# Two heads in one kernel (a Fourier mixing layer and a state-space convolution): seeds of two chunks of tables made together, inputs of the odd outputs made one group sooner

## The chip, the cores and the metric

The kernel runs on one core of one Trainium2 chip. The metric is the device time of one execution, in microseconds (us). A core has five engines that each take their instructions in a fixed order: PE (TensorE, matrix products), DVE (VectorE), ACT (ScalarE), POOL (GpSimd) and SP (SyncE, which here only issues transfers). They wait for each other through semaphores, and 16 DMA engines move data between DRAM (HBM) and the core's memory.

## The reference

Two independent heads are computed and laid side by side. Head A is the real part of a two-dimensional Fourier transform, by matrices; head B is a causal convolution along the sequence, by Fourier transforms of twice the length.

```python
# A: x is 1 x 2048 x 512
a = einsum("bsd,ed->bse", x, dft_hid_re);  b = einsum("bsd,ed->bse", x, dft_hid_im)
yA = einsum("ts,bse->bte", dft_seq_re, a) - einsum("ts,bse->bte", dft_seq_im, b)
# B: u is 1 x 2048 x 512; A, C are 512 channels x 128 modes, dt has 512 channels
P = exp((A * dt[:, None])[:, :, None] * arange(2048))         # 512 x 128 x 2048
K = 2 * einsum("dn,dnl->dl", C, P).real                       # a filter of 2048 taps per channel
yB = irfft(rfft(u, 4096) * rfft(K, 4096))[:2048] + u * D_skip
out = concatenate([yA, yB], axis=-1)                          # 1 x 2048 x 1024
```

## The kernel before, in words

**One program, planned ahead.** Two classes, `Fnet` (head A) and `Ssm` (head B), hold tasks written as generators. Each step of a task names an engine, a cost in us and perhaps an urgency; `Plan` runs the tasks against these costs while the program is built and so fixes the order of instructions on each engine. On the chip nothing is reordered: an instruction whose input is late holds up all that stand behind it on its engine. The constants at the file's end (`GROUP_US`, `AHEAD_US`, `SEEDS`, `ARGS` and others) and the costs in the steps therefore change the order, though they compute nothing.

**Head A.** The rows of x are folded by symmetry, so that 2048 output rows come in four quarters t = 0..3 (t = 2 and 3 hold the odd rows) with a sine part (c = 1) and a cosine part (c = 0). For each (t, c), called a group, `matmuls` and `sums` (L519 to L523) multiply the folded x by four "quads" of the sequence matrix S. A quad (`load_quad`) is 1 MB: a `base` of 256 KB and three `slots` tiles of 256 KB, which DVE turns into a bf16 `rest` (L414, L419). The loading of quads is paced by `loads`: quad n is held until `GROUP_US*(n//4) + QUAD_US*(n%4) - AHEAD_US`. After both parts of a quarter, `outputs` (L619, L620) applies the hidden matrix, 16 pairs of matmuls per quarter, and `evacuate` copies to `y` and stores `out_ya`. For t = 2 and 3 other foldings of x are needed: `load_odd(k)`, k = 0..3, loads x again into a `slots` tile, subtracts twice (L307), and `folded` makes the sine input "os" and the cosine input "oc" (L321 or L323, then L328). They overwrite the tiles of "es" and "ec" of quarter 1, so all four calls are made in `finish` of group (1, 0), after both parts of quarter 1 are through.

**Head B, tables.** The powers P are never formed in full. For 16 chunks of 32 channels, DVE makes two tables by repeated doubling: `tables1` (low powers times C, tiles t1) and `tables2` (powers of 32, tiles t2, with squares from ACT). All start from "seeds" `cs`, the powers 1, 2, 4, ... of one step, made per chunk: `load_par` fetches the chunk's parameters, `seed_args` computes arguments (five ACT copies L993 and L995, two DVE instructions L997 and L999), then ACT takes an exponential (L1003) and three sines (L1005, L1007, L1009), with a table load of ACT ahead of the exponential and ahead of the first sine; `seeds` multiplies them on DVE (L1018). The tile "seed" has one buffer, `cs` two.

**Head B, from tables to output.** `taps` (L1158) contracts t1 with t2 on PE to 2048 taps for each channel of a chunk; two chunks go through a first Fourier stage (`stage1_k`, L1234) to a spectrum `xk` in DRAM. The spectrum `xu` of u is made early. Channels are then taken in five units of 128, 128, 128, 64 and 64 (units 0 to 4), in quarters: 4, 4, 4, 2 and 2 of them. A quarter loads pieces of `xu` and `xk`, goes through PE (L1399), ACT (L1424), DVE (the complex product, two of L1429 and two of L1431) and PE again (L1445), and is stored to `zs`; `inverse` loads `zs`, runs L1516 and stores `out_yb`. Unit 4, the last 64 channels, needs the last two chunks: its spectrum does not go through DRAM, but stays in the tables' memory (`last_stage1_k`, L1206 and a DVE transpose L1212, then the DVE product L1417 and a transpose L1496). Unit 3 is marked late: DVE takes its products after the last table.

**The names used below.** "The end of tables" is the end of the last DVE instruction of L953, the last half of t1 of chunk 15. Behind it only head B's last units remain.

Of the kernel before, what the change touches and what calls it, by code (L numbers as in the profile page):

```python
# [57 lines left out]
ARGS = 0.3  # L58
# [138 lines left out]
class Fnet:  # L197
# [11 lines left out]
    def __init__(self, tc, ctx, plan, x, wT, sT, out):  # L209
# [5 lines left out]
        self.slots = Ring(self.slots_all[:, n] for n in range(SLOTS))  # L215
        self.ys = Sem(STAGED)
# [11 lines left out]
        self.checked, self.checks, self.odd_ev = Event(), 36, Event()  # L228
# [66 lines left out]
    def load_odd(self, k):  # L295
        nc = self.nc
        yield self.bases
# [12 lines left out]
        yield from self.folded("oc", k, raw[:, 0], raw[:, 1], OP.subtract, None if k else 1)  # L310
        self.ssm.give_tile(self.slots, raw)

    def folded(self, name, k, left, right, op, sign=None):

        nc, v, minus = self.nc, self.nc.vector, name[1] == "s"
# [4 lines left out]
        if sign is None:  # L320
            v.tensor_tensor(y, left, right, op=op)  # L321
        else:
            v.scalar_tensor_tensor(y, right, self.sign[:, sign:sign + 1], left, op0=OP.mult, op1=OP.add)  # L323
        n = 1 if minus else 2
# [45 lines left out]
    def loads(self, b):  # L370
# [3 lines left out]
        for n, i in enumerate(self.quads):  # L374
# [77 lines left out]
    def spare(self):  # L452
# [4 lines left out]
        self.ssm.give_tile(self.ssm.big, flat[:, :2048])  # L457
        self.ssm.give_tile(self.ssm.mid, flat[:, 2048:])
# [69 lines left out]
    def finish(self, t, c, bank, both):  # L528
# [186 lines left out]
class Ssm:  # L715


    def __init__(self, tc, ctx, plan, nd, ldt, dsk, uG, f1u, f1k, w2, ia, ib, ibl, out):
# [18 lines left out]
        self.t1_half, self.half_taps, self.last_xt, self.last_k, self.last_ib = (Event() for _ in range(5))  # L737
# [96 lines left out]
    def load_tables(self):  # L834
# [11 lines left out]
        first = self.tab.tile([128, 4, CHUNK], F32, name="par", bufs=2)  # L846
        yield self.pars
        self.rest, self.par = rest, {0: first}
# [56 lines left out]
    def setup_rest(self):  # L905
# [8 lines left out]
        self.par[1] = self.tab.tile([128, 4, CHUNK], F32, name="par", bufs=2)  # L914
        yield "act", act(4 * CHUNK)
        self.nc.scalar.activation(self.par[1], par[:, :, :CHUNK], AF.Copy)
# [9 lines left out]
    def load_par(self, ck):  # L926
        if ck == 1:
            yield self.par1_ev
            return
        yield self.par_ev  # L930
        yield self.pars
        self.par[ck] = self.tab.tile([128, 4, CHUNK], F32, name="par", bufs=2)
        o = CHUNK * ck - FIRST
        yield "dma", load(2 * CHUNK)
        self.nc.sync.dma_start(self.par[ck], self.par_dram[:, :, o:o + CHUNK])
# [45 lines left out]
    def seed_args(self, ck, box, ev):  # L981

        a, v = self.nc.scalar, self.nc.vector
        if ck:
# [640 lines left out]
```

## Time and profile before

| what | value |
|---|---|
| median of 3 runs (lowest, highest) | 488.81 us (486.59, 490.38) |
| time of the profiled execution | 487.21 us |
| span of the profiled execution, first to last instruction | 485.1 us |
| granted PE clock, mean | 0.961 |
| busy: PE, DVE, ACT | 397.4, 428.5, 347.4 us |
| DMA | 110.49 MB, mean 228 GB/s |

The span is what the trace shows; the time has 2.1 us more around it. Busy is time in which an engine worked; the rest of the span it waited. "A <- B" names what an engine waited for. In a timeline a row is a stretch of equal instructions: start in us from the span's start, length in us, engine, line, operation, output tile <- input tiles, shapes, count, and in brackets the idle time ahead of it with what ended it. A float32 matmul of the program stands as two in the trace.

### The profile page before, as it was taken

How to read it: one execution, taken by the hardware profiler on the slowest of the kernel's cores; microseconds unless marked ns; L12 is line 12 of the kernel's file. 1: busy time of each engine (PE TensorE's matmuls, PEld its weight loads, DVE VectorE, ACT ScalarE, POOL GpSimd, SP SyncE). 2: the span in 40 equal slices, each digit the busy share in tenths (PEclk: the TensorE clock that was granted, in tenths of full speed). 3: DMA queues.
4: the chain of work that ended last, by engine and by line, in shares of the span. 5: the costliest groups of instructions: out<-in, count | busy, mean ns of one | idle time of the engine just before them, and what ended most of it. 6: DMA issues, size and time to landing. Idle time of an engine off the chain costs nothing. (4 is left out here: it accounts for less than half of the span.)

```text
span 485.1 us, 13793 instructions
## 1 busy us (share of the span) xinstructions
PE 397.4 (82%) x5744; PEld 213.3 (44%) x5778; DVE 428.5 (88%) x732; ACT 347.4 (72%) x687; POOL 1.3 (0%) x15
## 2 busy tenths in 40 slices
PE   4548958999998695798897799998976989886593
PEld 3113214354534352453445254644343556665383
DVE  3999997989999999989999999999999999982433
ACT  1529899899998884669858988887897754633331
POOL 1000000000000000000000000000000000000000
PEclk9988987999999998999999999999999999997888
DMA  8998894895976379994986279449301995998674
GB/s 308 340 295 297 291 330 139 295 329 189 278 281 214 139 204 322 336 286 154 284 258 235 61 232 309 141 119 329 87 3 49 251 296 165 288 253 195 220 198 112
DMA packets 130546, 110.49 MB, mean 228 GB/s; under 512 B 57136, under 2 KB 101552, under 8 KB 129968
## 3 DMA queue, kind: packets, MB, share of 16 engines
q1 hardware_dynamic: 122512, 106.55, 70.1%
q10 hardware_dynamic: 7968, 3.02, 2.4%
q8 instruction: 47, 0.77, 0.7%
q14 instruction: 19, 0.16, 0.1%
HBM read 77.11 MB, written 32.44 MB: 226 GB/s over the span
## 5 line engine op out<-in xcount | busy, mean ns | idle before, releaser
L944 DVE TENSOR_TENSOR prod<-tables,cs 128x1024 f32<-128x1024 f32 (+4 forms) x160 | 124.6, 798 | 3.7 <-ACT tables L1087 2.3
L619 PE MATMUL f<-p,w 128*128 128x512 f32 x128 | 67.7, 610 | 8.9 <-ACT y L645 5.8
L953 DVE TENSOR_TENSOR tables<-prod 128x512 f32<-128x512 f32 (+4 forms) x160 | 74.0, 477 | 0.8
L443 ACT ACTIVATE slots<-rest 128x1536 f32<-128x1536 bf16 x32 | 47.4, 1480 | 16.3 <-DVE rest L414 13.8
L414 DVE TENSOR_TENSOR rest<-slots,base 128x512 bf16<-128x512 f32 (+2 forms) x52 | 53.8, 1034 | 1.9 <-DMA slots<-in_sT 1.8
L1158 PE MATMUL f<-tables 128*32 128x96 f32 x2048 | 47.0, 247 | 9.2 <-ACT big L808 2.8
L1158 PEld LDWEIGHTS f<-tables 128*32 128x32 f32 x2048 | 42.6, 110 | 18.6 <-issue 6.0
L520 PE MATMUL f<-base,es 128*128 128x512 f32 x64 | 36.9, 660 | 15.5 <-ACT es L331 7.2
L1110 DVE TENSOR_TENSOR tables<-tables,cs 128x1024 f32<-128x1024 f32 x32 | 38.0, 1220 | 0.0
L619 PEld LDWEIGHTS f<-p,w 128*128 128x128 f32 x128 | 22.5, 189 | 32.0 <-issue 16.0
L520 PE MATMUL f<-base,ec 128*128 128x512 f32 x64 | 34.3, 618 | 1.2 <-ACT big L1424 0.8
L523 PE MATMUL f<-rest,xi 128*128 128x512 bf16 x87 | 26.2, 397 | 5.7 <-ACT xi L273 2.5
L1399 PE MATMUL f<-big,w 64*32 64x256 f32 (+1 forms) x768 | 23.7, 380 | 6.1 <-DMA big<-xk 5.1
L1424 ACT ACTIVATE big<-f 128x1024 f32<-128x1024 f32 x22 | 21.9, 1020 | 7.8 <-PE f L1399 3.9
L808 ACT ACTIVATE big<-f 128x512 f32<-128x512 f32 x39 | 21.0, 588 | 7.2 <-PE f L1516 7.2
L523 PE MATMUL f<-rest,xr 128*128 128x512 bf16 x92 | 25.2, 379 | 0.6 <-DVE rest L414 0.4
L967 ACT ACTIVATE tables<-tables 128x1024 f32<-128x1024 f32 x16 | 16.8, 1050 | 10.5 <-PE f L1158 8.4
L1234 PE MATMUL f<-ks,f1k 32*128 32x512 f32 (+1 forms) x224 | 22.4, 499 | 2.3 <-ACT ks L1182 1.5
L523 PEld LDWEIGHTS <-xi 128*128 128x128 bf16 x96 | 9.5, 101 | 30.1 <-issue 21.8
L520 PEld LDWEIGHTS f<-base,es 128*128 128x128 f32 x64 | 11.8, 203 | 24.6 <-ACT es L331 10.5
L1023 ACT ACTIVATE cs<-cs 128x352 f32<-128x352 f32 x32 | 15.8, 530 | 9.0 <-DVE cs L1018 8.9
L1399 PEld LDWEIGHTS f<-big,w 64*32 64x32 f32 x768 | 14.0, 111 | 15.9 <-issue 10.6
(187 smaller groups left out, 732.7 us busy)
## 6 DMA issues: line engine op xcount, KB each, us to landing
slots<-in_sT SPq DMA_DIRECT2D x31, 768.0 KB, 6.0
xu<-big SPq DMA_DIRECT2D x16, 512.0 KB, 4.1
base<-in_sT SPq DMA_DIRECT2D x31, 256.0 KB, 6.2
xk<-big SPq DMA_DIRECT2D x7, 1024.0 KB, 6.8
big<-xu SPq DMA_DIRECT2D x11, 512.0 KB, 7.7
big<-xk SPq DMA_DIRECT2D x11, 512.0 KB, 7.3
zs<-mid SPq DMA_DIRECT2D x10, 512.0 KB, 6.2
big<-zs SPq DMA_DIRECT2D x10, 512.0 KB, 7.0
```

What stands on the lines that cost most here:

```text
L414: return v.tensor_tensor(rest[:, lo:hi:step], raw[:, lo:hi:step], base[:, None, :].to_broadcast([128, n, DM]), op=op)
L443: nc.scalar.activation(raw, rest, AF.Square, accum_out=self.stat[:, n:n + 1])
L520: nc.tensor.matmul(out, x[:, cols], base, start=k == 0, stop=False)
L523: nc.tensor.matmul(out, still[:, cols], rest[:, h], start=False, stop=k == 3 and h == 2)
L619: nc.tensor.matmul(ps, self.w[k][:, cols], self.p[t, c][:, d], start=k == 0, stop=False)
L944: self.nc.vector.tensor_tensor(p.rearrange("p k d c m -> p k (d c) m"), src.rearrange("p d c l -> p (d c) l")[:, None, :, rows].to_broadca ...
L953: self.nc.vector.tensor_tensor(dst[:, :, :, rows], p[:, 0], p[:, 1, :, ::-1], op=OP.add)
L1110: self.nc.vector.tensor_tensor(self.top[:, :, k, ::1 - 2 * k, 16:32], t[:, :, :, 1:32:2], cs[:, k, 5, :, :, None].to_broadcast([128, CHUNK ...
L1158: nc.tensor.matmul(ps[32 * j:32 * j + 32, i], t1[:, d, c], t2[:, :, d, c], start=c == 0, stop=c == 1, tile_position=(0, 32 * j))
L1234: nc.tensor.matmul(to, self.f1k[r, STEPS[a]], taps, start=a == 0, stop=a == 4, tile_position=(32 * j, 0))
L1399: nc.tensor.matmul(both[:, :, c], self.w2[rows, R * q + r, xx, 32 * c:32 * c + 32], xs[rows, r, xx], start=True, stop=True, tile_position= ...
L1424: a.activation(flat[:, 1024 * m:1024 * m + 1024], p.rearrange("p b d -> p (b d)"), AF.Copy)
```

## The change

- **Seeds of two chunks together.** A table `PAIRS` groups the 16 chunks as 0; 1 and 2; 3 and 4; ...; 13 and 14; 15. `load_par` and `seed_args` run once for a pair, on tiles of double width; `seeds` still runs once per chunk, on half of the pair's tile. The tiles "par" and "seed" are twice as large. `f1k_last` has no buffer of its own any more; it takes the buffer "square" after that one's last use.
- **x for odd t a group sooner.** `load_odd` is now spawned in `finish` of group (1, 1), when only "es" is free. It makes "os" as before. "oc" has no free tile yet: its first DVE step works in place in the `slots` tile, the result is stored to DRAM (`oc`, 256 KB for each k), and a new task `load_oc`, spawned in `finish` of group (1, 0), loads it into a `y` tile and makes the rest.
- **Pace of S and urgencies.** `GROUP_US` 42 to 43, `AHEAD_US` 25 to 35; `ARGS` 0.3 to 1; `SEEDS` 0.5 to 1.5; planned cost of `taps` 2.45 to 2.8 (last chunk 1.25 to 1.42 a half).

```diff
-ARGS = 0.3
+ARGS = 1
     def load_odd(self, k):
         nc = self.nc
+        yield self.even_ev
         yield self.bases
...
         yield from self.folded("os", k, raw[:, 1], raw[:, 0], OP.add, None if k else 0)
-        yield from self.folded("oc", k, raw[:, 0], raw[:, 1], OP.subtract, None if k else 1)
+        yield "dve", dve(512)
+        if k:
+            nc.vector.tensor_tensor(raw[:, 0], raw[:, 0], raw[:, 1], op=OP.subtract)
+        else:
+            nc.vector.scalar_tensor_tensor(raw[:, 0], raw[:, 1], self.sign[:, 1:2], raw[:, 0], op0=OP.mult, op1=OP.add)
+        yield "dma", load(256)
+        nc.sync.dma_start(self.oc[k], raw[:, 0])
         self.ssm.give_tile(self.slots, raw)
+        self.plan.set(self.oc_ev[k])
+
+    def load_oc(self, k):
+        yield self.oc_ev[k]
+        yield self.ys
+        y = self.pool.tile([128, DM], F32, name="y", bufs=STAGED)
+        yield "dma", load(256)
+        self.nc.sync.dma_start(y, self.oc[k])
+        yield from self.fold("oc", k, y)
...
             elif n == 16:
+                self.plan.set(self.even_ev)
                 yield self.odd_ev
...
-            if (t, c) == (1, 0):
-                self.plan.spawn(self.load_odd(k), 0)
+            if t == 1:
+                self.plan.spawn(self.load_odd(k) if c else self.load_oc(k), 0)
...
+    def take_pair(self, g):
+        first, m = PAIRS[g]
+        self.pair[g] = self.tab.tile([128, 4, 2 * CHUNK], F32, name="par", bufs=2)[:, :, :m * CHUNK]
+        for j in range(m):
+            self.par[first + j] = self.pair[g][:, :, CHUNK * j:CHUNK * j + CHUNK]
...
-    def seed_args(self, ck, box, ev):
+    def seed_args(self, g, box, ev):
...
-        s = self.tab.tile([128, 3, 11, CHUNK], F32, name="seed")
+        s = self.tab.tile([128, 3, 11, 2 * CHUNK], F32, name="seed")[:, :, :, :w]
...
-    def seeds(self, ck, s):
+    def seeds(self, g, j, s):
         yield self.css
+        s = s[:, :, :, CHUNK * j:CHUNK * j + CHUNK]
...
-        self.plan.put(self.res)
+        if j == PAIRS[g][1] - 1:
+            self.plan.put(self.res)
...
-            yield "pe", 2.45, None, 257
+            yield "pe", 2.8, None, 257
...
-        self.f1k_last = self.tab.tile([128, 3, 128], F32, name="f1k_last")
+        yield self.squared
+        self.f1k_last = self.tab.tile([128, 512], F32, name="square")[:, :384].rearrange("p (e s) -> p e s", e=3)
...
+PAIRS = ((0, 1), *((n, 2) for n in range(1, 15, 2)), (15, 1))
-FIRST_TABLE, T1, SEEDS = 0.01, 0.005, 0.5
+FIRST_TABLE, T1, SEEDS = 0.01, 0.005, 1.5
-GROUP_US, QUAD_US, AHEAD_US = 42, 11, 25
+GROUP_US, QUAD_US, AHEAD_US = 43, 11, 35
```

The planner's new order moves much more than the diff says. Three places follow. The changed file is longer, so its lines have other numbers there: L944, L953, L1158, L1206, L1212, L1399, L1429, L1431 of before are L980, L989, L1200, L1248, L1254, L1442, L1472, L1474.

The first place is DVE at the end of tables. Before, from the last table (the second row here) on:

```order
L944 TENSOR_TENSOR prod<-tables,cs 128x1024
L953 TENSOR_TENSOR tables<-prod 128x32x16
L1429 TENSOR_TENSOR mid_106<-slots 128x512
L1212 STREAM_TRANSPOSE tables<-f_4486 128x2x8x32
L1431 TENSOR_TENSOR slots<-slots 128x2x256
L1212 STREAM_TRANSPOSE tables<-f_4487 128x2x8x32
L1429 TENSOR_TENSOR mid_106<-slots 128x512
L1431 TENSOR_TENSOR slots<-slots 128x2x256
L1212 STREAM_TRANSPOSE tables<-f_4553 128x2x8x32
L1212 STREAM_TRANSPOSE tables<-f_4588 128x2x8x32
L1429 TENSOR_TENSOR slots<-big_103 128x512
L1431 TENSOR_TENSOR big_103<-big_103 128x2x256
```

With the change, at the same place (the last table is the sixth row):

```order
L1254 STREAM_TRANSPOSE tables<-f_4482 128x2x8x32
L980 TENSOR_TENSOR prod<-tables,cs 128x1024
L1254 STREAM_TRANSPOSE tables<-f_4529 128x2x8x32
L989 TENSOR_TENSOR tables<-prod 128x32x16
L980 TENSOR_TENSOR prod<-tables,cs 128x1024
L989 TENSOR_TENSOR tables<-prod 128x32x16
L1472 TENSOR_TENSOR slots<-slots 128x512
L666 COPY y<-f_4266 128x256
L1474 TENSOR_TENSOR slots<-slots 128x4x128
L1472 TENSOR_TENSOR slots<-slots 128x512
L1474 TENSOR_TENSOR slots<-slots 128x4x128
```

A shape ending in 2x256 is a quarter of unit 2, one in 4x128 a quarter of unit 3: before, the last two quarters of unit 2 stand behind the end of tables; now they stand ahead of it, and two of unit 4's transposes too, while the copy of head A's last output (L666, before at L639) has gone behind it.

The second place is PE ahead of the last chunk's taps (the row with L1158 or L1200). Before, head A had ended earlier:

```order
L1158 MATMUL f_4369<-tables 32x96 x64
L1399 MATMUL f_4375<-slots,w_95 32x2x128 x16
L1399 MATMUL f_4411<-slots,w_95 32x2x128 x16
L1206 MATMUL f_4486<-ks,f1k_last 128x256 x2
L1206 MATMUL f_4487<-ks,f1k_last 128x256 x2
```

With the change, directly ahead of the last chunk's taps:

```order
L646 MATMUL f_4266<-p_3685,w_438 128x512
L647 LDWEIGHTS v_481
L647 MATMUL f_4266<-low_3706,v_481 128x512
L646 MATMUL f_4266<-p_3141,w_507 128x512
L647 LDWEIGHTS v_555
L647 MATMUL f_4266<-low_3239,v_555 128x512
L1442 MATMUL f_4534<-slots,w_98 32x2x64 x32
L1442 MATMUL f_4563<-slots,w_98 32x2x64 x32
L646 MATMUL f_4266<-p_3141,w_585 128x512
L647 LDWEIGHTS v_610
L647 MATMUL f_4266<-low_3239,v_610 128x512
L1200 MATMUL f_4573<-tables 32x96 x64
```

The matmuls of head A's last output tile (L646, L647, before at L619, L620) now stand between the taps of chunks 14 and 15, and the first quarter of unit 3 (shape 32x2x64) has come ahead of the last taps.

The third place is SP where x for odd t is loaded. Before:

```order
L935 DMA par<-par_dram 128x4x32
L764 DMA ib<-in_ib 128x2048
L304 DMA slots<-in_x 128x512 x3
L304 DMA base<-in_x 128x512
L304 DMA slots<-in_x 128x512 x3
L304 DMA base<-in_x 128x512
L935 DMA par<-par_dram 128x4x32
L648 DMA out_ya<-y 128x512
L796 DMA xk_83<-big_102 4096x1x64
L304 DMA slots<-in_x 128x512 x3
L304 DMA base<-in_x 128x512
```

With the change, at the last two of the four x (their loads are above these rows; L319 stores oc, L329 loads it again, L423 and L425 load the first quads of S for odd t):

```order
L319 DMA oc<-slots 128x512
L675 DMA out_ya<-y 128x512
L1410 DMA big_106<-xu 128x8x128
L319 DMA oc<-slots 128x512
L1410 DMA big_106<-xk_86 128x8x128
L675 DMA out_ya<-y 128x512
L329 DMA y<-oc 128x512
L423 DMA base<-in_sT 128x512
L425 DMA slots<-in_sT 128x3x512
L329 DMA y<-oc 128x512
L423 DMA base<-in_sT 128x512
L425 DMA slots<-in_sT 128x3x512
```

Four stores and four loads of 256 KB have come into the SP queue, two of the loads behind a gather of `xk` (512 KB) and ahead of the quads that the odd groups wait for.

More of the change, by code (lines that the diff above doesn't have):

```diff
@@ L456, in spare @@
         flat = self.slots_all.rearrange("p n h t -> p (n h t)")
[L457 to L458 removed]
+        n = 3 * DM * SLOTS // 2048
+        for m in range(n):
+            self.ssm.give_tile(self.ssm.big, flat[:, 2048 * m:2048 * m + 2048])
+        for m in range(2 * n, 3 * DM * SLOTS // 1024):
+            self.ssm.give_tile(self.ssm.mid, flat[:, 1024 * m:1024 * m + 1024])
     def first(self):
@@ L931, in load_par @@
         yield self.pars
[L932 to L935, printed above, removed]
+        self.take_pair(g)
+        first, m = PAIRS[g]
+        o = CHUNK * first - FIRST
+        yield "dma", load(2 * m * CHUNK)
+        self.nc.sync.dma_start(self.pair[g], self.par_dram[:, :, o:o + m * CHUNK])
     def mul(self, name, src, rows, seed):
@@ L1065, in tables1 @@
             self.nc.scalar.activation(t[:, :, :, 0].rearrange("p d c -> p c d"), self.par[n][:, 2:4], AF.Copy)
-            self.plan.put(self.pars)
+            if any(n == first + m - 1 for first, m in PAIRS):
+                self.plan.put(self.pars)
             for j in range(4):
```

59 lines of the change are left out of this document (34 added, 25 removed).

## The prediction

> **What bounds the kernel now.** First the busy time by engine on the page, then the same by stage. In the stage rows the columns are PE, PEld, DVE, ACT and POOL busy (with instruction counts), granted PE clock, DMA share and GB/s.
>
> ```profile
> PE 397.4 (82%) x5744; PEld 213.3 (44%) x5778; DVE 428.5 (88%) x732; ACT 347.4 (72%) x687; POOL 1.3 (0%) x15
> 40.00:400.00 360.00, 314.25 (x3857) 154.88 (x3888) 346.00 (x591) 299.44 (x593) 0.00 (x0) 0.98 0.71 223
> 388.10:423.90 35.80, 32.08 (x736) 21.86 (x737) 35.11 (x66) 20.81 (x36) 0.00 (x0) 1.00 0.81 249
> 425.80:485.10 59.30, 40.56 (x1256) 32.20 (x1256) 25.77 (x35) 18.76 (x31) 0.00 (x0) 0.86 0.74 195
> ```
>
> From 40 to 400 us DVE works 346.00 of 360 us. PE and ACT have 46 and 61 us to spare. So up to the end of tables the kernel is DVE's queue, and any work or wait put into that queue is paid in full. From 425.8 us on DVE works 25.77 of 59.30 us: that is another regime, which I call the tail. Next the DVE timeline, for where the regimes meet and for the prices of what the order moves across that point:
>
> ```profile
> 403.28 0.42 DVE L639 COPY y<-f 128x256 f32<-128x256 f32 x1
> 407.10 0.67 DVE L1429 TENSOR_TENSOR mid<-big 128x512 f32<-128x512 f32 x1
> ...
> 409.75 0.15 DVE L481 TENSOR_SCALAR small<-small 1x2 f32<-1x2 f32 x1
> 425.09 0.69 DVE L953 TENSOR_TENSOR tables<-prod 128x512 f32<-128x512 f32 x1
> 430.10 2.07 DVE L1212 STREAM_TRANSPOSE tables<-f 128x512 f32<-128x512 f32 x2
> 450.26 0.69 DVE L1429 TENSOR_TENSOR prod<-tables 128x512 f32<-128x512 f32 x1 [10.12 <-ACT tables L1424]
> ```
>
> The tables end at 425.09 + 0.69 = 425.78 us; the tail is 485.10 - 425.78 = 59.3 us. The row at 450.26 shows DVE idle for 10.12 us: in the tail the products go round PE, ACT, DVE and PE. PE's timeline says what that takes.
>
> ```profile
> 423.95 1.53 PE L1158 MATMUL f<-tables 128*32 128x96 f32 x64 [0.86 <-DVE tables L953]
> 430.00 1.96 PE L1399 MATMUL f<-big,w 64*32 64x256 f32 x64
> 442.11 1.56 PE L1445 MATMUL f<-slots,ia 32*64 32x256 f32 x21 [3.69 <-issue]
> 447.44 2.59 PE L1399 MATMUL f<-tables,w 64*32 64x128 f32 x165
> 457.72 2.00 PE L1445 MATMUL f<-prod,ia 32*64 32x256 f32 x28 [2.92 <-issue]
> 460.45 1.98 PE L1516 MATMUL f<-big,ib 128*64 128x128 f32 x16 [0.73 <-ACT prod L808]
> 465.37 1.09 PE L1516 MATMUL f<-big,ib 128*64 128x128 f32 x16
> 466.39 1.21 PE L1445 MATMUL f<-tables,ia 32*64 32x256 f32 x32
> 467.31 1.16 PE L1445 MATMUL f<-prod,ia 32*64 32x256 f32 x32
> 468.39 1.09 PE L1516 MATMUL f<-slots,ib 128*64 128x128 f32 x16
> ```
>
> After the last taps and L1206, at 430.00 us, PE still has unit 2 to finish before it gets to the second quarter of unit 3 at 447.44 us. "issue" means that PE's own sequencer had nothing ready: 3.69 and 2.92 us here.
>
> **The change part by part.** *Seeds by pairs.* The price of one set, and of wider ones:
>
> ```profile
> L817 DVE TENSOR_SCALAR tables<-tables 128x480 f32<-128x480 f32 x1 | 0.4, 410 | 0.0
> L997 DVE TENSOR_SCALAR seed<-seed 128x352 f32<-128x352 f32 x16 | 5.4, 338 | 2.2 <-ACT seed L995 2.2
> L999 DVE TENSOR_TENSOR seed<-seed 128x352 f32<-128x352 f32 x16 | 8.3, 520 | 0.0
> L1018 DVE TENSOR_TENSOR cs<-seed 128x704 f32<-128x704 f32 x16 | 14.3, 891 | 0.4 <-ACT seed L1009 0.4
> L1005 ACT ACT_TABLE_LOAD x16 | 20.5, 1283 | 0.2
> L1003 ACT ACT_TABLE_LOAD x15 | 19.2, 1283 | 0.3
> L1003 ACT ACTIVATE seed<-seed 128x352 f32<-128x352 f32 x16 | 7.9, 497 | 0.2
> L967 ACT ACTIVATE tables<-tables 128x1024 f32<-128x1024 f32 x16 | 16.8, 1050 | 10.5 <-PE f L1158 8.4 <-DVE tables L953 2.1
> ```
>
> 16 sets become 9, so 7 are saved. On ACT, 672 more elements cost 1050 - 497 = 553 ns, 0.82 ns each, which leaves 497 - 290 = 207 ns fixed per instruction; a set has 10 of them and two table loads, so 7 x (10 x 0.207 + 2 x 1.283) = 32.5 us leave ACT. ACT is not what DVE's queue waits for as a rule, so only DVE's own waits for it can come back. On DVE a pair costs 891 for the difference (L1018 has the size) and 338 + 352 x (410 - 338) / 128 = 536 ns for L997, against 2 x 858: 0.29 us saved, 7 times 2.0 us, all on the path. **-2.0.** DVE's waits from 40 us to the end of tables:
>
> ```profile
> DVE prod L944 <- ACT tables L1087: 2.3, 1, 2.3
> DVE seed L997 <- ACT seed L995: 2.2, 3, 0.9
> DVE tables L979 <- ACT square L960: 0.9, 2, 0.7
> DVE y L321 <- ACT bec L332: 0.6, 1, 0.6
> DVE cs L1018 <- ACT seed L1009: 0.4, 1, 0.4
> ```
>
> Those for ACT are 6.4 us together. A freer ACT can take away between none and all; sets that are twice as long can also come late. I take **-2.0** (0 to -6.4). The cover of the longer set is one chunk: "seed" comes free when the second chunk's `cs` is made, and the next set (10 instructions on ACT, none longer than the 1.05 us of L967, and two table loads: under 13.1 us) is due one chunk later, which is about 385 / 16 = 24 us of DVE.
>
> *x for odd t.* DVE runs the same 16 instructions for it; SP gets 8 transfers of 256 KB more and 7 of the "par" loads fewer. What waits is the second step of "oc" on DVE, for a round trip:
>
> ```profile
> out_ya<-y SPq DMA_DIRECT2D x15, 256.0 KB, 5.9
> base<-in_x SPq DMA_DIRECT2D x4, 256.0 KB, 5.9
> big<-xk SPq DMA_DIRECT2D x11, 512.0 KB, 7.3
> ```
>
> A store and a load of this size land after 5.9 us each, 11.8 us in sequence. In DVE's new order 12 to 13.5 us of other work, summed from the mean rows, stand between the first step of each k and its second. So it is hidden, barely; if a load waits for a gather ahead of it (7.3), it is not. Behind those loads on SP stand the first two quads of odd t, whose `rest` follows on DVE within 16 us. That x comes a group sooner moves PE's odd groups forward, but not DVE's total: worth nothing by itself. The Trainium skill, "DMA: Bandwidth & Descriptors", section "Anatomy of one DMA", gives a transfer about 2 us fixed and the rest at some 436 GB/s. By that a round trip would be an estimated 5.2 us, and no wait could arise; the rows above say twice that on this loaded queue, and I go by them.
>
> *Pace of S.* Quads are held 9 us less at first (10 of head start, less 1 per group) and 3 us less at the end. Only two `slots` tiles exist, so the loads still go by DVE's pace. 0.
>
> *The order.* Ahead of the end of tables come two quarters of unit 2, each 409.75 - 407.10 = 2.65 us on DVE: **+5.3**; two transposes: **+2.1**; one copy leaves: **-0.4**. On PE, between the taps of chunk 13 and those of chunk 15 (the 35.80 us stage above, 32.08 busy), I count four more pairs of head A's output matmuls (1.17 us each, row below), one more L1399 (1.96), two more L1445 (2.0 each, 466.39 to 468.39) and four fewer halves of L1516 (1.09): 32.08 + 6.3 = 38.4 us of work, where DVE has 35.11 + 5.0 = 40.1.
>
> ```profile
> 386.92 1.02 PE L619 MATMUL f<-p,w 128*128 128x512 f32 x2
> 387.78 0.38 PE L620 MATMUL f<-low,v 128*128 128x512 bf16 x1
> 388.09 2.85 PE L1158 MATMUL f<-tables 128*32 128x96 f32 x128
> ```
>
> That leaves PE 2 us, and its own waits in this stage were 35.80 - 32.08 = 3.7 us. DVE now waits for it in two transposes. For new waits on DVE, here and at "oc", I take **+4** (0, if all covers hold, to 25 in the rival below). The end of tables: -2.0 - 2.0 + 5.3 + 2.1 - 0.4 + 4 = +7.0, at 432.8 us.
>
> *The tail.* The second quarter of unit 3 now follows L1206 directly: 430.00 - 425.78 = 4.2 us after the end of tables. Before it began at 447.44, and 485.10 - 447.44 = 37.7 us followed. What follows is the same work (last quarter of unit 3, unit 4, four halves of unit 2's inverse), plus one L1445 of unit 3's first quarter, 2.2 us. The tail becomes 4.2 + 37.7 + 2.2 = 44.1 us, with the stalls of before left in: **-15.2**. Without the stall of 2.92 us and with the 1.8 us of rival (c) it would be 39.4; that is the low end (-19.9). The high end is -10, if further stalls of 2.92 and 2.2 us come in.
>
> **Sum.** +7.0 - 15.2 = -8.2 us: span 476.9, time 479.0 against 487.21. The profiled execution lies 1.6 us under the median of the three runs, 488.81; on that scale I predict **480.6 us**.
>
> **Rivals.** (a) *PE becomes the bound ahead of the tables' end.* For: only 2 us of room, with fetch stalls of 0.9 to 3.7 us seen on "issue". Against: head A's outputs wait for nothing from the tables. Two or three such stalls, some 7 us more than my 4, and half the tail's gain filled with them would leave -1: 487, within 1%.
>
> (b) *Slower: the round trip of "oc" stops DVE.* With a gather ahead the trip is 5.9 + 5.9 + 7.3 = 19.1 us, against 12 to 13.5 us of cover: up to 6.5 us for each of four, 25 us in all, and every table behind it is that late. It decides from 4 + 8.2 + 4.9 = 17 us of waits on. At 19 us: 480.6 + 15 = 496. Against: the four trips go in two pairs, and the second of a pair waits little.
>
> (c) *The tail runs at full clock.* PE's clock in the tail was 0.86. The L1516 group of 16 took 1.98 us at 460.45 and 1.09 at 465.37, so slow rows stand behind the 3.69 and 2.92 us gaps. The Trainium skill, "TensorE: Matmul & The Clock Gate", Part 1, says that the clock is throttled unless PE was busy for some 3.4 us, and that gaps bring the throttle back. The rows agree. If PE now has work through the gaps, the rows at 457.72 (2.00 for 28, against 1.16 for 32) and 460.45 each lose 0.9 us, both within the 37.7 us of the sum: 1.8 us. Time: 478.8.
>
> (d) *It does nothing:* the tail might be set by the transfers of the last units and not by PE. The gap of 10.12 us on DVE waits for ACT, which waits for PE, so I give this no chance of its own.
>
> **Chances.** My sum 0.45, (c) 0.12, (a) 0.20, (b) 0.23. For this kernel 1% is about what a measurement can tell from no change: 483.9 to 493.7 us. Faster: 0.45 + 0.12 = 0.57, less 0.02 for the sum's upper edge, 0.55. Same: 0.20 + 0.02 = 0.22. Slower: 0.23. The range reaches from the low ends of ACT's and the tail's terms together with no new waits (480.6 - 4.4 - 4.7 - 4 = 467.5, taken as 469, since all three at once are unlikely) to the middle of (b), 495. The sum's own range is 473 to 486.
>
> **What would show it.** End of tables in the DVE timeline: 430 to 436 us. Tail from there: 42 to 47 us. ACT busy about 315 us. In DVE's waits, "ec <- DMA y" of a few us at most; over 10 means (b). In PE's waits ahead of the end of tables, "issue" over 5 us means (a). The forecast is wrong if the tail stays over 50 us, or if DVE idles over 25 us between 40 us and the end of tables.

## The result and the profile after

| | before | after |
|---|---|---|
| median of 6 runs each (lowest, highest) | 488.96 us (486.59, 491.31) | 481.58 us (477.93, 485.28) |
| ratio of after to before, 95% interval | | 0.9845 [0.9803, 0.9887] |
| time, span of the profiled execution | 487.21, 485.1 us | 483.77, 482.0 us |
| end of tables | 425.79 us | 433.66 us |
| tail, from there to the end | 59.31 us | 48.31 us |
| DVE work, DVE idle up to the end of tables | 402.7, 23.1 us | 406.9, 26.7 us |

The change makes the kernel 1.5% faster; 480.6 us was forecast. The last three rows are worked out from the trace: DVE's instructions up to the last one of L953 (L989 after), overlaps counted once, and what is left of that time. They stand for every kernel below. The profiled execution of after lies 2.2 us over its median, that of before 1.7 us under its own, so the two traces differ by 3.4 us where the medians differ by 7.4: the terms below are read for their places, and the medians decide on sums. Nor is a tail sharper than some 3 us: act_filled and trip_3 below keep the order of after and change nothing behind its tables, and had 46.5 and 45.3 us where after had 48.31.

First the busy time by engine, and two stages of after, up to 400 us and behind the end of tables (columns as in the prediction):

```profile
PE 404.6 (84%) x5735; PEld 214.5 (45%) x5778; DVE 426.0 (88%) x718; ACT 322.0 (67%) x603; POOL 1.3 (0%) x15
40.00:400.00 360.00, 320.15 (x4003) 160.93 (x4046) 343.30 (x580) 276.72 (x512) 0.00 (x0) 0.96 0.76 234
433.70:482.00 48.30, 31.45 (x959) 24.75 (x947) 19.08 (x26) 13.01 (x23) 0.00 (x0) 0.85 0.60 169
```

DVE is still the queue of the first 400 us (343.30 of 360). In the tail PE has 31.45 us of work where it had 40.56, at a granted clock of 0.85 as before (0.86). Next DVE at the point where the regimes meet:

```profile
432.97 0.69 DVE L989 TENSOR_TENSOR tables<-prod 128x512 f32<-128x512 f32 x1
439.61 2.03 DVE L1254 STREAM_TRANSPOSE tables<-f 128x512 f32<-128x512 f32 x2 [3.08 <-PE f L1248]
446.94 0.69 DVE L1472 TENSOR_TENSOR mid<-big 128x512 f32<-128x512 f32 x1 [3.69 <-ACT big L1467]
...
461.45 0.69 DVE L1460 TENSOR_TENSOR prod<-f,tables 128x512 f32<-128x512 f32 x1 [5.99 <-ACT tables L1457]
```

The tables end at 432.97 + 0.69 = 433.66 us, and the idle gap of 10.12 us that DVE had ahead of unit 3's second quarter is now 3.69 (the row at 446.94). Ahead of the second quarter of unit 4 DVE still waits 5.99 us, where it waited 9.52 before; that is the longest gap left in the tail. DVE's waits from 40 us to the end of tables:

```profile
DVE tables L1148 <- PE f L1200: 5.1, 4, 2.2
DVE cs L1055 <- ACT seed L1045: 2.5, 2, 1.4
DVE prod L980 <- ACT tables L1127: 1.2, 1, 1.2
DVE tables L1015 <- ACT square L996: 1.0, 2, 0.5
DVE ec L351 <- DMA y<-oc: 0.2, 1, 0.2
```

With two rows of 0.9 and 0.2 that are not shown the waits for ACT are 5.8 us, against 6.4 before: the freer ACT gave almost none of them back. Those for PE grew from 1.7 to 5.1 us. The wait for the way by DRAM is 0.2 us. Its transfers (median us to landing in the last column) were shorter than the 5.9 us taken for them:

```profile
oc<-slots SPq DMA_DIRECT2D x4, 256.0 KB, 2.5
y<-oc SPq DMA_DIRECT2D x4, 256.0 KB, 3.8
```

The whole way was no shorter, though. By SP's timeline each load was issued 2.7 to 10.0 us behind the landing of its store, because SP had others to issue first and waited for them (once 4.1 us for DVE's second step of the `oc` before, once 3.7 for a store of `out_ya`). From the issue of the store to the landing of the load the four ways took 12.0, 15.7, 11.0 and 12.2 us, where 11.8 had been forecast. The first load landed 3.7 us before DVE needed it, the second held DVE up, the other two came 0.1 and 0.7 us before: three of the four covers were all but used up.

Last, PE's timeline of the tail, for where it still stands:

```profile
431.82 0.57 PE L1200 MATMUL f<-tables 128*32 128x96 f32 x17 [0.42 <-DVE tables L989]
432.96 1.19 PE L1200 MATMUL f<-tables 128*32 128x96 f32 x47 [0.57 <-issue]
435.64 1.53 PE L1200 MATMUL f<-tables 128*32 128x96 f32 x64 [1.49 <-ACT ks L1224]
437.84 1.61 PE L1248 MATMUL f<-ks,square 32*128 32x256 f32 x32 [0.67 <-ACT ks L1224]
439.50 1.73 PE L1442 MATMUL f<-big,w 64*32 64x128 f32 x103
444.74 1.08 PE L1442 MATMUL f<-big,w 64*32 64x128 f32 x25 [3.50 <-issue]
445.75 3.72 PE L1488 MATMUL f<-slots,ia 32*64 32x256 f32 x64
...
456.68 1.12 PE L1488 MATMUL f<-big,ia 32*64 32x256 f32 x32
...
468.60 1.15 PE L1559 MATMUL f<-tables,ib 128*64 128x64 f32 x32 [1.29 <-DMA tables<-zs]
471.21 1.85 PE L1559 MATMUL f<-tables,ib 128*64 128x64 f32 x32 [1.45 <-DMA tables<-zs]
```

The second quarter of unit 3 begins at 439.50, 5.8 us after the tables; before it began 21.7 us after them (447.44 - 425.78). That is where the tail becomes shorter. What works against it: a wait of 1.49 us for ACT between the halves of the last taps, a gap of 3.50 us on "issue" within that very quarter, and a slow clock behind the gap (64 in 3.72 us at 445.75, 32 in 1.12 at 456.68: 1.5 us lost; the granted clock was 0.50 from 444.75 to 449.40 and 1.00 from 456.70 to 459.60).

### The profile page after: what moved, and what is told of

Same layout as the page of the kernel before. It is cut to its first block, busy times and chain, and to the rows that moved or that the text cites. A ratio compares the mean times of both kernels' runs of the same rounds, so it can differ in the third digit from the quotient of the medians.

```text
span 482.0 us, 13688 instructions
## 1 busy us (share of the span) xinstructions
PE 404.6 (84%) x5735; PEld 214.5 (45%) x5778; DVE 426.0 (88%) x718; ACT 322.0 (67%) x603; POOL 1.3 (0%) x15
## 5 line engine op out<-in xcount | busy, mean ns | idle before, releaser
L980 DVE TENSOR_TENSOR prod<-tables,cs 128x1024 f32<-128x1024 f32 (+4 forms) x160 | 124.3, 796 | 2.8 <-ACT tables L1127 1.2
L646 PE MATMUL f<-p,w 128*128 128x512 f32 x128 | 69.2, 622 | 5.8 <-ACT y L672 5.4
L989 DVE TENSOR_TENSOR tables<-prod 128x512 f32<-128x512 f32 (+4 forms) x160 | 72.3, 475 | 0.7
L467 ACT ACTIVATE slots<-rest 128x1536 f32<-128x1536 bf16 x32 | 47.4, 1482 | 22.9 <-DVE rest L438 15.5
L1200 PE MATMUL f<-tables 128*32 128x96 f32 x2048 | 49.4, 257 | 3.7 <-ACT ks L1224 1.5
L1200 PEld LDWEIGHTS f<-tables 128*32 128x32 f32 x2048 | 45.6, 116 | 11.9 <-issue 5.1
L547 PE MATMUL f<-base,es 128*128 128x512 f32 x64 | 38.9, 692 | 12.8 <-ACT xi L275 6.4
L646 PEld LDWEIGHTS f<-p,w 128*128 128x128 f32 x128 | 22.7, 193 | 30.4 <-issue 17.5
L550 PE MATMUL f<-rest,xi 128*128 128x512 bf16 x86 | 28.3, 426 | 8.8 <-DVE rest L438 2.6
L1467 ACT ACTIVATE big<-f 128x1024 f32<-128x1024 f32 x24 | 23.6, 1022 | 14.5 <-PE f L1442 14.5
L835 ACT ACTIVATE big<-f 128x512 f32<-128x512 f32 x36 | 20.0, 594 | 14.7 <-PE f L1276 7.7
L1442 PE MATMUL f<-big,w 64*32 64x256 f32 (+1 forms) x832 | 24.4, 367 | 5.1 <-issue 3.5
L550 PE MATMUL f<-rest,xr 128*128 128x512 bf16 x85 | 24.1, 380 | 0.5
L996 ACT ACTIVATE square<-tables 128x256 f32<-128x256 f32 (+1 forms) x32 | 16.6, 517 | 10.1 <-DVE tables L989 9.9
L1442 PEld LDWEIGHTS f<-big,w 64*32 64x32 f32 x832 | 14.9, 107 | 14.1 <-issue 6.3
```

Of the source, the lines that this page charges most:

```text
L467: nc.scalar.activation(raw, rest, AF.Square, accum_out=self.stat[:, n:n + 1])
L547: nc.tensor.matmul(out, x[:, cols], base, start=k == 0, stop=False)
L550: nc.tensor.matmul(out, still[:, cols], rest[:, h], start=False, stop=k == 3 and h == 2)
L646: nc.tensor.matmul(ps, self.w[k][:, cols], self.p[t, c][:, d], start=k == 0, stop=False)
L980: self.nc.vector.tensor_tensor(p.rearrange("p k d c m -> p k (d c) m"), src.rearrange("p d c l -> p (d c) l")[:, None, :, rows].to_broadca ...
L989: self.nc.vector.tensor_tensor(dst[:, :, :, rows], p[:, 0], p[:, 1, :, ::-1], op=OP.add)
```

## The experiments

All times are set against runs of before on the same chip. T0 is the end of tables.

| kernel | median us | ratio [95%] | T0 | tail | DVE work, idle to T0 |
|---|---|---|---|---|---|
| single_seeds | 499.21 | 1.0231 [1.0171, 1.0292] | 441.9 | 55.7 | 411.7, 30.3 |
| late_oddx | 484.87 | 0.9957 [0.9914, 1.0001] | 433.9 | 52.7 | 407.8, 26.1 |
| old_pace | 489.21 | 1.0029 [0.9994, 1.0064] | 434.3 | 55.5 | 406.5, 27.8 |
| unit2_late | 487.55 | 1.0012 [0.9974, 1.0051] | 420.1 | 63.3 | 397.0, 23.1 |
| act_filled | 505.37 | 1.0317 [1.0255, 1.0380] | 456.8 | 46.5 | 407.5, 49.2 |
| pairs_alone | 489.40 | 1.0007 [0.9978, 1.0036] | 433.8 | 53.7 | 408.0, 25.8 |
| oddx_alone | 503.04 | 1.0296 [1.0251, 1.0341] | 441.0 | 60.8 | 407.0, 34.0 |
| pace_alone | 499.66 | 1.0233 [1.0187, 1.0278] | 449.2 | 47.6 | 410.8, 38.4 |
| none_of_three | 510.51 | 1.0430 [1.0376, 1.0483] | 438.4 | 71.0 | 407.2, 31.2 |
| pace_on_before | 489.64 | 1.0021 [0.9990, 1.0053] | 438.7 | 50.3 | 410.4, 28.4 |
| trip_3 | 499.38 | 1.0212 [1.0157, 1.0268] | 453.9 | 45.3 | 407.3, 46.6 |
| taps_2p9 | 485.78 | 0.9948 [0.9914, 0.9982] | 436.1 | 51.4 | 408.7, 27.4 |

The theory at the start was the prediction's own: the time comes from where the new order puts quarters of unit 2, DVE's work ahead of T0 against PE's work behind it. Its rival: it comes from what the seeds leave of ACT and so from DVE's waits. One warning holds for all but act_filled and trip_3: each edit changes the planner's costs or events, so the whole order is dealt anew.

**One part taken back at a time.** single_seeds has one chunk per set; late_oddx has the old way of x for odd t; old_pace has the five old constants.

```diff
 single_seeds
-        self.nc.scalar.activation(self.pair[1], par[:, :, :2 * CHUNK], AF.Copy)
+        self.nc.scalar.activation(self.pair[1], par[:, :, :PAIRS[1][1] * CHUNK], AF.Copy)
...
-PAIRS = ((0, 1), *((n, 2) for n in range(1, 15, 2)), (15, 1))
+PAIRS = tuple((n, 1) for n in range(16))
```

> The changed kernel with one chunk of seeds at a time again (16 sets, double tiles unused). In its order no quarter of unit 2 stands behind the end of tables, as in the changed kernel. Theory 'quarters' (the gain comes from where the order puts unit 2's quarters; a freer ACT is worth 2 us at most): 482 to 485 us, ratio to before 0.985 to 0.993, tail 46 to 50 us, ACT busy about 350 us. Rival 'ACT' (the 32 us taken from ACT are the gain): ratio 0.997 or more. Rival 'early x': 0.985, as with the change.

```diff
 late_oddx
-        yield self.even_ev
...
+        yield from self.folded("oc", k, raw[:, 0], raw[:, 1], OP.subtract, None if k else 1)
...
-            if t == 1:
-                self.plan.spawn(self.load_odd(k) if c else self.load_oc(k), 0)
+            if (t, c) == (1, 0):
+                self.plan.spawn(self.load_odd(k), 0)
```

> The changed kernel with x for odd t loaded as before, after group (1, 0), and no way through DRAM. Its order has no quarter of unit 2 behind the end of tables, but three of head A's last four output pairs on PE behind the start of the last taps. 'Quarters': 482 to 486 us, ratio 0.986 to 0.995, tail 48 to 53 us. 'ACT': 0.985. 'Early x': 0.997 or more.

```diff
 old_pace
-ARGS = 1
+ARGS = 0.3
-            yield "pe", 2.8, None, 257
+            yield "pe", 2.45, None, 257
-                yield "pe", 1.42, None, 129
+                yield "pe", 1.25, None, 129
-FIRST_TABLE, T1, SEEDS = 0.01, 0.005, 1.5
+FIRST_TABLE, T1, SEEDS = 0.01, 0.005, 0.5
-GROUP_US, QUAD_US, AHEAD_US = 43, 11, 35
+GROUP_US, QUAD_US, AHEAD_US = 42, 11, 25
```

> The changed kernel with the constants of before (pace of S 42/25, urgencies 0.3 and 0.5, taps planned at 2.45). No quarter of unit 2 behind the end of tables, but eight output pairs of head A on PE behind the start of the last taps, 1.17 us each: 9.4 us on PE in the tail, some of it in stalls. 'Quarters': 484 to 488 us, ratio 0.990 to 0.998, end of tables about 2 us sooner than with the change, tail 52 to 57 us. 'ACT' and 'early x': 0.985.

Single seeds cost 17.6 us against after, the old pace 7.6, the old way of x 3.3. The theory of the quarters had given single_seeds up to 0.993, old_pace up to 0.998 and late_oddx up to 0.995, and each came out above, late_oddx only just; so in the changed code it does not account for the gain by itself. For single seeds the rival's row (0.997 or more) is the one that holds. The loss in single_seeds is in three places: 4.8 us more DVE work ahead of T0, 3.6 us more idle time there, and a tail 7.4 us longer. What DVE's rows for seeds could give (2 us) is not near it. DVE's waits in single_seeds up to T0, with those for ACT's seeds now first among the waits for ACT:

```profile
DVE seed L1033 <- ACT seed L1031: 2.7, 2, 1.9
DVE cs L1055 <- ACT seed L1045: 2.6, 4, 1.2
DVE prod L980 <- ACT tables L1127: 2.4, 2, 1.2
DVE tables L1015 <- ACT square L996: 1.9, 5, 0.6
```

With one row of 0.7 not shown these waits for ACT are 10.3 us, against 5.8 in after. The part that was forecast at 4 us gives the most, and only partly by what the prediction named.

**The quarters alone.** unit2_late is after with unit 2 marked late as unit 3 is, so that its four quarters follow the last table.

```diff
-LATE, BIGS = ((0, 128), (128, 128), (256, 128), (384, 64), (448, 64)), (3,), 3
+LATE, BIGS = ((0, 128), (128, 128), (256, 128), (384, 64), (448, 64)), (2, 3), 3
```

> The changed kernel with unit 2 marked late as unit 3 is: all four of its quarters stand behind the end of tables. 'Quarters': the tables end about 9 us sooner (DVE has 400.2 us of work ahead of it instead of 409.9), and the tail, which lost 11 us with two quarters, gains 22 us with four: 70 us; 494 us in all, ratio 1.008 to 1.018. Rival 'tail set by transfers of the last units' (the number of quarters is hidden): tail 48 to 55 us, 472 to 479 us, ratio 0.966 to 0.980.

T0 came 13.5 us sooner and the tail grew by 15.0 us, in the stage behind T0 mostly with PE's work, 44.92 us for 31.45:

```profile
420.12:483.40 63.28, 44.92 (x1408) 34.32 (x1400) 29.04 (x41) 21.42 (x35) 0.00 (x0) 0.88 0.79 199
```

Both moves have the forecast's direction. What is left is small: 1.4 us by the two spans, 6.0 by the medians, less than the 7.8 us (15.2 - 5.3 - 2.1) that the prediction gave for half as many quarters. The expectation of 1.008 to 1.018 was not reached: the trade of DVE work ahead of T0 for PE work behind it is real, but worth less than forecast.

**ACT's room, with the order kept.** act_filled is after with 18 needless ACT copies of 64 columns behind the last sine of each pair, which the planner is not told of. Nothing is left out.

```diff
         a.activation(k, k, AF.Sin, scale=-TWO_PI, bias=self.halfpi)
+        fill = self.tab.tile([128, 64], F32, name="fill")
+        for _ in range(18 * PAIRS[g][1] - 18):
+            a.activation(fill, self.halfpi.to_broadcast([128, 64]), AF.Copy)
```

> The changed kernel with its order kept, and 18 needless ACT copies of 64 columns behind each pair's last sine: about the 32 us of ACT time that the pairs saved are put back (their result is used by nothing). If ACT's room is worth what DVE no longer waits for, 2 to 6 us come back ahead of the end of tables and none in the tail: 484 to 488 us, ratio 0.988 to 0.998. If the single seeds' loss (18 us) was ACT's load as such: 490 us or more, ratio over 1.00. If ACT's room is worth nothing: 482, ratio 0.985.

T0 came 23.1 us later at the same DVE work, ratio 1.0317. From 40 to 400 us ACT had 83 us to spare in after; the copies stand in the way of what DVE needs next:

```profile
DVE tables L1015 <- ACT square L996: 12.9, 5, 3.9
DVE prod L980 <- ACT tables L1130: 6.0, 1, 6.0
DVE mid L1475 <- ACT big L1470: 4.5, 1, 4.5
```

Work on ACT that comes in one piece at a wrong place is thus paid for on DVE. The ratio falls in the row "ACT's load as such" (over 1.00), but the load alone does not set the price: ACT is busy 352.2 us here and 349.6 in single_seeds, whose tables end 8.3 us later than after's and not 23.1. Nor is it proof that taking such work away gains as much: the copies stand behind the seeds in bulk, which single sets do not.

**One part alone, in the changed code.** Each is after with the other two parts taken back by the edits above.

```diff
 pairs_alone: the edits of late_oddx and old_pace
 oddx_alone:  the edits of single_seeds and old_pace
 pace_alone:  the edits of single_seeds and late_oddx
```

> The kernel before with pairs of seeds alone; x for odd t, pace and urgencies as before. By the sum seen so far (end of tables = DVE work ahead of it + 23 to 30 us of waits; tail = PE work in it + about 26 us): DVE 407 + 26 = 433, PE in the tail 26.0 + 26 = 52: span 485, time 487 us, ratio 0.990 to 1.002. Theory 'pairs alone bring it': 0.985.

> The kernel before with x for odd t a group sooner alone (one chunk of seeds at a time, old pace). Two quarters of unit 2 stand behind the end of tables, as before. Sum: DVE 403 + 25 = 428, PE in the tail 32.1 + 26 = 58: span 486, time 488 us, ratio 0.992 to 1.004. Theory 'early x brings it': 0.985.

> The kernel before with the new pace, urgencies and planned cost of taps alone (one chunk of seeds at a time, x for odd t as before). Sum: DVE 409 + 28 = 437, PE in the tail 24.0 + 26 = 50: span 487, time 489 us, ratio 0.994 to 1.008; with single seeds at this pace DVE may wait more, as it did in the run of single seeds with the early x. Theory 'the pace brings it': 0.985.

None gains against before: 1.0007, 1.0296, 1.0233. Only pairs_alone lies within its expected range (0.990 to 1.002); the other two came out 2.6 and 1.5% above theirs. pace_alone has the short tail of after (47.6 us) but its tables end 15.5 us later than after's; most of it idle time of DVE (11.7 us), and its waits are spread over ACT's results:

```profile
DVE prod L972 <- ACT tables L1119: 4.2, 3, 1.8
DVE cs L1047 <- ACT seed L1037: 3.9, 4, 1.4
DVE seed L1025 <- ACT seed L1023: 2.2, 1, 2.2
```

**The control: no part at all, in the changed code.** none_of_three has all the edits of single_seeds, late_oddx and old_pace. It differs from before only in what the change left around its parts: buffers for two chunks, `f1k_last` in "square", memory given back in other pieces, planned costs of the seeds.

> The code of after with all three parts taken back: one chunk per set of seeds, x for odd t in one step and where it was, the old constants. It computes what before computes, but the tiles of the changed code (the copies of `par` and the buffers given back at the end) make the planner deal another order: by mean rows 404.9 us of DVE work ahead of the end of tables, and 36.9 us of PE work behind it, against 403.1 and 32.1 in before. Theory 1 (the three parts make the time through DVE's idle time; single seeds are only dear together with the new pace or the early x): DVE idles as in before, 23 to 27 us, end of tables 428 to 432, tail 36.9 + 22 to 28 = 59 to 65, ratio 1.005 to 1.02. Theory 2 (luck of the dealt order: single seeds in the changed code are dear by themselves): DVE idles 30 us or more, end of tables 435 to 440, ratio 1.02 to 1.04.

510.51 us, 22 us over before, though the three parts are as in before. Its tail is 71.0 us, PE with 51.7 us of work in it:

```profile
438.35:509.30 70.95, 51.71 (x1349) 37.10 (x1348) 23.86 (x38) 20.02 (x33) 0.00 (x0) 0.88 0.72 193
```

By its 31.2 us of idle time and T0 of 438.4 this is the second theory's case, the luck of the dealt order; the ratio is just above that theory's 1.04. So an order dealt anew can cost as much as any part gains, and a ratio of "one part alone" to before says little about the part.

Among kernels of one code the eight combinations can be compared. Pairs gain in all four settings of the other two: 21.1 us (none_of_three to pairs_alone), 13.8, 14.8 and 17.6. The pace gains 10.8, 4.5, 3.8 and 7.6. The early x gains 7.5, 0.2, 0.5 and 3.3. With pairs T0 is 433.7 to 434.3 us in all four, without them 438.4 to 449.2; DVE idles 25.8 to 27.8 us with them and 30.3 to 38.4 without. On average over the four settings pairs take 6.9 us of idle time, 1.9 us of work and 6.2 us of tail away (the medians of before beside these runs differ by up to 1.2 us). DVE's waits for ACT, from 40 us to T0, are 3.9 to 7.5 us in the four kernels with pairs and 9.8 to 12.4 in the four without, 5.0 us less on average: most of the idle time saved is waiting for ACT. So neither theory is the whole: the idle time, which goes with ACT's room, is nearly half, and the shorter tail, which the order deals, nearly the other. The tail's share goes from 17.3 us less to 5.1 us more, the idle time's from 3.6 to 12.3 us less: only the latter has one sign.

**The same on the code of before.** pace_on_before is before with only the five constants.

```diff
-GROUP_US, QUAD_US, AHEAD_US = 42, 11, 25
+GROUP_US, QUAD_US, AHEAD_US = 43, 11, 35
...
```

`ARGS`, `SEEDS` and the planned costs of taps are changed too, as in the change.

> The kernel before with only the five constants of the pace: single sets of seeds, x for odd t in one step. By mean rows DVE has 409.9 us of work ahead of the end of tables, PE 24.0 us behind it: the same two sums as in after. So the place of the quarters is as in after, and only ACT's load and the way of x differ. If the place of the quarters makes the gain by itself: end of tables 432 to 437, tail 46 to 50, ratio 0.98 to 0.99. If the new place can only be held with the room that paired seeds give ACT: DVE idles 33 to 40 us, with waits for ACT over 10 us, end of tables 443 to 450, tail 46 to 50, ratio 1.01 to 1.025, as in the run with the pace alone in the changed code.

1.0021: no gain, though the quarters now stand as in after. The tail is 9.0 us shorter, T0 12.9 us later: DVE has 7.7 us more work ahead of it and idles 5.3 us more. Its waits for ACT and PE grew:

```profile
DVE prod L944 <- ACT tables L1087: 4.3, 3, 2.5
DVE tables L1106 <- PE f L1158: 3.7, 2, 2.0
DVE cs L1018 <- ACT seed L1009: 2.3, 3, 1.6
```

It fell between both expectations (T0 438.7). The same parts in the changed code, pace_alone, took 10 us more, with another order again and the changed code's buffers.

**A neighbour of after.** taps_2p9 changes one planned cost.

```diff
-            yield "pe", 2.8, None, 257
+            yield "pe", 2.9, None, 257
```

> After with one constant changed, what the planner thinks a run of taps costs PE (2.8 to 2.9). By mean rows DVE's work ahead of the end of tables and PE's work behind it stay 409.9 and 24.0 us, but 14 instead of 9 pairs of output matmuls stand between the taps of chunk 13 and the last ones. If the two sums make the time: end of tables 432 to 436, tail 46 to 50, ratio 0.98 to 0.99. If the gain hangs on how single pieces fall: another end of tables by 5 us or more, ratio 0.995 or above. If PE's work between the taps bounds (rival (a)): waits of DVE for PE over 8 us, end of tables 438 to 441, ratio 0.99 to 1.0.

0.9948: by the ratios two thirds of the gain are gone, while the two sums are the same by mean rows (the trace has 408.7 us of DVE work ahead of T0 and 35.0 of PE work behind it, after 406.9 and 31.5). What differs for PE is that 14 pairs of output matmuls, not 9, stand between the taps of chunk 13 and the last ones. PE's timeline shows them as its backlog, and DVE's the end of tables:

```profile
436.90 0.38 PE L647 MATMUL f<-low,v 128*128 128x512 bf16 x1
437.12 1.02 PE L646 MATMUL f<-p,w 128*128 128x512 f32 x2
437.98 0.38 PE L647 MATMUL f<-low,v 128*128 128x512 bf16 x1
438.28 1.53 PE L1200 MATMUL f<-tables 128*32 128x96 f32 x64
...
444.35 1.72 PE L1442 MATMUL f<-big,w 64*32 64x128 f32 x100
```

```profile
435.43 0.69 DVE L989 TENSOR_TENSOR tables<-prod 128x512 f32<-128x512 f32 x1
```

The tables end at 436.12, and PE turns to the last taps only at 438.28; in after it began them at 431.82, before T0. Five pairs at 1.40 us are 7.0 us, and the last taps come 6.5 us later. DVE's waits for PE are 8.5 us, as rival (a), PE as the bound ahead of T0, would have them, and the time is near the price that the prediction gave it (487; 485.8 measured). T0 is not: 436.1, where 438 to 441 was expected. late_oddx shows the same backlog: its last taps begin at 438.77, 4.8 us after its tables. But in both kernels the orders of DVE and ACT differ from after's in other places too, so that the output pairs cost all of it is argued, not shown.

**The way by DRAM, three times as long.** trip_3 is after with each load of `oc` done three times in a row; the order is the same and nothing is left out.

```diff
-        self.nc.sync.dma_start(y, self.oc[k])
+        for _ in range(3):
+            self.nc.sync.dma_start(y, self.oc[k])
```

> After, with each of the four loads of the cosine part out of DRAM done three times in a row into the same tile, each behind the one before; the order is the same, nothing is left out. A load takes about 3.8 us here, so each second step on DVE comes 7.6 us later, and SP stands 7.6 us longer at each. In after one of the four second steps waited 0.21 us: its cover was used up, and the others had some microseconds left. Rival (b) of the prediction, that each late microsecond is paid in full: waits of DVE for y 10 to 20 us, or the same in waits for the loads behind them on SP, end of tables 444 to 454, ratio 1.005 to 1.03. If DVE's queue makes the delay good again (the work that waits would have waited for something else): waits of 5 to 10 us, end of tables 434 to 440, ratio 0.985 to 0.995.

1.0212; T0 is 20.2 us later, 19.9 of it idle time of DVE. Its waits:

```profile
DVE ec L352 <- DMA y<-oc: 16.1, 4, 5.2
DVE tables L1149 <- PE f L1201: 6.6, 5, 2.5
DVE rest L439 <- DMA slots<-in_sT: 3.5, 3, 1.7
```

Rival (b) is real as a mechanism: 16.1 us of waits, and nothing behind them made them good. In after the way took about as long as forecast (11.0 to 15.7 us), and it was hidden by luck more than by room: two loads landed 0.1 and 0.7 us before DVE needed them, a third 0.2 us late.

## Why the prediction was right, step by step

The forecast, faster by the exchange of a later T0 for a shorter tail, holds: T0 +7.9 us (forecast +7.0), tail -11.0 in the profiled execution (forecast -15.2, range -10 to -19.9), median 481.58 for 480.6. The nearness of the last two numbers is in part luck. In the traces the two terms add up to -3.1 us, not -8.2; only the medians give -7.4. And the prediction left -4.2 us to the trade of quarters and waits for the tail (+7.0 + 4 - 15.2) and -4.0 to the pairs of seeds, while on the code of before the trade alone brought nothing (pace_on_before, 1.0021) and in the changed code the pairs brought 13.8 to 21.1: as far as these kernels tell, one term was too large and the other too small.

- *Seeds on DVE, -2.0.* By their rows 5.4 + 8.3 = 13.7 us became 11.5, so -2.2. Right:

```profile
L1033 DVE TENSOR_SCALAR seed<-seed 128x704 f32<-128x704 f32 x7 | 3.6, 519 | 0.2 <-ACT seed L1031 0.2
L1033 DVE TENSOR_SCALAR seed<-seed 128x352 f32<-128x352 f32 x2 | 0.7, 352 | 0.0
L1035 DVE TENSOR_TENSOR seed<-seed 128x704 f32<-128x704 f32 x7 | 6.2, 883 | 0.0
L1035 DVE TENSOR_TENSOR seed<-seed 128x352 f32<-128x352 f32 x2 | 1.0, 519 | 0.0
```

- *ACT saved, 32.5 us.* Summed over the rows of the seeds ACT has 32.4 us less; its busy time on the page fell by 25.4, to 322.0 instead of about 315.
- *ACT room, -2.0.* The step that was mis-sized. DVE's waits for ACT went from 6.4 to 5.8 us, a gain of 0.6 against before. Against the same code without pairs DVE idles 3.6 to 12.3 us less. The prediction priced the room by the waits that before had, not by those that the new order would have without it.
- *Quarters, transposes and copy, +7.0 of DVE work, with the seeds +5.0.* DVE's work up to T0 grew by 4.2. Right.
- *New waits, +4.* Those for PE rose by 3.4, that for `oc` is 0.2. Right in sum. For `oc` the prediction took transfers of 5.9 us in direct sequence; they took 2.2 to 5.6 us, with 2.7 to 10.0 us between store and load that the sum left out. Three times the load made 16 us of waits. The prediction's other estimate, 5.2 us and no wait, did not hold either: the two transfers of a way took 5.7 to 9.3 us together. The section of the Trainium skill that it rests on ("DMA: Bandwidth & Descriptors", "Anatomy of one DMA") is on transfers that GpSimd issues, and these are issued by SP.
- *x for odd t, nothing by itself; pace of S, 0.* Next to pairs the early x gained 0.2 and 3.3 us, the pace 4.5 and 7.6, in kernels whose orders differ as well. Neither makes DVE's work less. On the code of before the pace alone moves the quarters (pace_on_before), so 0 was only right for its loads; in the changed code they stand ahead of T0 with the old pace too (old_pace).
- *The tail, 44.1 us.* Right in mechanism, mis-sized by 4.2. The quarter of unit 3 began 5.8 us after T0, not 4.2 (+1.6: the first half of the last taps, with a gap of 0.57 in it, ended 0.5 us after T0 and not 0.3 before it, and the wait for ACT behind it was 1.49 us for 0.66). From there 482.0 - 439.50 = 42.5 us followed, not 39.9 (+2.6): the added L1488 took 3.72 us at half the clock, not 2.2, and PE's idle time was 14.7 us, not 13.6. Waits of 1.29 and 1.45 us for `zs` came in, while the gaps on "issue" were a little shorter in sum.
- *Rival (c), full clock in the tail.* It didn't happen: 0.85.
- *The prediction's signs.* T0 within 430 to 436 and the wait for `oc` under a few us, as named; the tail 48.3, above its 42 to 47 but under 50. DVE idled 17.8 us between 40 us and T0, under the 25 named. PE's waits on "issue" in the last 36 us ahead of T0 were 0.6 us, so the sign of rival (a) did not show in after.

What stays open: how the 7.4 us divide among the parts on the code of before. The nearest chain is pace_on_before (1.0021), then pairs and early x with the same sums by mean rows (taps_2p9, 0.9948), then five output pairs out of the way (after, 0.9845). Each step lies outside the other's interval, but these orders differ in details too. That the idle time which pairs save is due to ACT's being on time is argued from waits and idle times of eight kernels with different orders; a kernel in which ACT's load alone goes down, with the order held, was not tried. So that pairs gain is shown by four comparisons in the changed code; the way in which they do is in part argued.

## What to carry to other kernels

Where an order is planned ahead, test a part against a control that has the new code without the part: here that control was 4.3% slower than the old kernel, and every "one part alone" looked like a loss or nothing. Price a freed engine not by the waits of the old order but by those that the new order would have without the room. And before the last stage, count what the engine of that stage still has queued ahead of it: with five more pairs of 1.40 us ahead of the last taps two thirds of the gain were gone (taps_2p9).

## What was not expected of the hardware

- The 256 KB transfers of `oc` took 2.5 and 3.8 us to landing, where the other groups of that size in the same program took 2.6 to 6.4. The 5.9 us from before's rows were too long for that place. But each load was issued only 2.7 to 10.0 us behind the landing of its store: here the way by DRAM cost its place in SP's queue too.
- In the tail of each of after, taps_2p9, pace_on_before and none_of_three a group of many small matmuls is cut by a gap of 2.1 to 3.5 us on "issue" (3.50 within L1442 here), and the rows behind some of the gaps run at about half speed, with a granted clock of 0.50. The traces tell what ends such gaps. The profile's pages list a queue "q8 instruction", in each trace 47 packets of 16 KB. Of the 47 gaps of PE on "issue" over 1.2 us, behind the first 40 us of all fourteen traces, 45 end 1.1 to 1.8 us after such a packet has come in (the 3.50 us here 1.4 us after); of the 209 gaps of that length that end otherwise, 12 do. So PE seems to wait there for its next instructions. Why they come late at these places no run here tells.
- ACT at 67% busy can still set DVE's pace: 18 short copies behind each pair put 23.1 us on T0 (act_filled).
